# A gated mix of linear attention and an MLP: the denominators' sums by exchanges of partitions on VectorE

## The chip, the core and the metric

The kernel runs on one core of a Trainium2 chip. The metric is the device time of one launch in microseconds. Engines by the names of the profile: PE is TensorE's matrix products, PEld its weight loads, DVE is VectorE, ACT is ScalarE, POOL is GpSimd, SP is the queue that starts most of the DMAs.

## The reference

Everything is float32. With x of 2048 rows and 448 columns, 16 heads of 28 columns, and an MLP of 1792 hidden columns:

```
g = sigmoid((x * gate_w).sum(-1))
q, k, v = x @ wqkv                       per head, 28 columns each
phi(t) = where(t > 0, t + 1, exp(t)) + 1e-6
kv = phi(k)^T v ;  z = sum over rows of phi(k)
a = ((phi(q) kv) / (phi(q) . z + 1e-6)) @ wo
b = relu(x @ w1 + b1)^2 @ w2 + b2
out = g * a + (1 - g) * b
```

What matters here is the denominator `phi(q) . z + 1e-6`: for each row of x and each head, a sum over the head's 28 columns.

## The kernel before

**Precision.** Each operand of a product is kept as two rounded parts, a high one (name ending in h) and a low one (l), made by `split_hi` (L63, a copy that rounds, on ScalarE or VectorE) and `split_lo` (L71, value minus high part, on VectorE or GpSimd). A product of two split operands is three products on TensorE: h with h, h with l, l with h. All add up in one PSUM bank.

**Tiling.** The 2048 rows are four blocks of 512 (`TB`), b = 0 to 3. The hidden columns are 14 groups of 128, f = 0 to 13. `up` (L241) makes one group of a block: 11 products of 512 columns into `h_ps`, then `hidden` (L231) empties it: ScalarE's relu with bias (L233) and square (L234) make `hr`, VectorE's cast (L69) makes `hh` and its subtraction (L72) `hl`. `down` (L260) multiplies `hh`, `hl` with w2 and adds into four `o_ps` banks, 12 products of 448 columns; with `leave` the last few are owed and run behind the next `up`, so that TensorE has work while a split is under way. The first product of a group reads `hh`, the third `hl`.

**First half** (L538 to L681): groups 0 to 6 for the blocks in turn, with the keys, their sums, and the product of keys and x from which, between the halves, the values' part is made. During it the mask `hm` (L664, L665) is loaded and rounded: 128 by 128, a one where two partitions belong to one head.

**Second half** (L684 to L771): groups 7 to 13 for the blocks in the order 3, 0, 1, 2; these four rounds are called the first to fourth pass here. Beside a pass's groups run the queries of the next block and the attention of this block:

- `queries` (L449 on): phi(q) for 512 rows as four tiles `qe` of 128 partitions, each from 11 products (7 for the fourth) into a bank `q_ps`. ScalarE's exp (L286) and VectorE's `qr` (L287) both read the bank; L288 joins them. The fourth tile holds only half as many columns, in two copies, and goes through DMAs that swap halves (`qv`, `qr`, L472 to L479). Each tile is multiplied with z, one number to a partition, and added into `ds` (L466, L468).
- The columns of q are dealt so that a head's part of `ds` lies in eight partitions of the same 32: those that agree in all bits of the partition's number but the bits 1, 2 and 16. The denominator is the sum over these eight.
- `split_den` (L483) splits `ds` into `dh` (ScalarE) and `dl` (VectorE). `denominators` (L489) multiplies both with the mask on TensorE: two products of 512 columns into the bank `d_ps`, which put the sum over a head's eight partitions into each of the eight. ScalarE adds 1e-6 on its way out (L494), and VectorE takes four reciprocals of 128 columns each (L498), in the next round of `run_todo`.
- `scaled` (L501): each tile `qe` times the reciprocals (L506), then split into `qh` and `ql`; the last tile by `split_last` (L76), which is longer.
- `attention` (L513): 11 products with `m_s` into a bank `a_ps` for each 128 rows; emptied by ScalarE (`u`, L525) and added to the rest by VectorE (L526). The tiles of q are taken in their order, so the last tile's `qh` and `ql` are used by the tenth and eleventh product.
- `finish` (L275): VectorE's L278 makes 128 rows of `out`, and SP sends them.

`q_ps`, `d_ps` and `a_ps` share two PSUM banks that alternate (`bank`, L48): each new tile waits until the tile two before it has been read out.

**What sets the order.** The order on TensorE, ScalarE and VectorE is the program's (L170): each runs its instructions in the order of the text, and waits at the first whose data are not there. Steps put on the list `todo` run in the next `run_todo` (L530), ahead of the next group's `up`.

Of the kernel before, what the change touches and what calls it, by code (L numbers as in the profile page):

```python
# [7 lines left out]
F = mybir.dt.float32  # L8
R = mybir.dt.float32r
AF = mybir.ActivationFunctionType  # L10
# [5 lines left out]
P = 128  # L16
# [12 lines left out]

@with_exitstack  # L30
def gated_mix_kernel(ctx: ExitStack, tc: tile.TileContext, xw, xt, xn, wk, wq, wv, wo, w1a, w1b, w2, b1, b2, gw,
                     hmask, kvmask, halves, out):
    nc = tc.nc
    act, dve, pool, pe, sp = nc.scalar, nc.vector, nc.gpsimd, nc.tensor, nc.sync

# [18 lines left out]
    def slot(shape, dt, name):  # L54
        return work.tile(shape, dt, name=name, tag="s", bufs=NSLOT)
# [7 lines left out]
    def split_hi(eng, hi, src):  # L63
        if eng is act:
            act.activation(hi, src, AF.Copy)  # L65
        elif eng is pool:
            pool.tensor_scalar(hi, src, 1.0, 0.0, op0=ALU.mult, op1=ALU.add)
        else:
            eng.tensor_copy(hi, src)  # L69

    def split_lo(eng, lo, src, hi):  # L71
        eng.tensor_tensor(lo, src, f32(hi), op=ALU.subtract)  # L72
# [131 lines left out]

    b2_s = keep.tile([P, D], F, name="b2_s")
    gw_s = keep.tile([P, D], F, name="gw_s")
    hm = keep.tile([P, 8 + P], R, name="hm")[:, 8:]
    dve.memset(ones, 1.0)
    ksum = keep.tile([P, D], F, name="ksum")

# [269 lines left out]
            after()  # L480
        return [swap if c == 3 else after]

    def split_den(b):  # L483
        den[b, "h"], den[b, "l"] = slot([P, TB], R, f"dh{b}"), slot([P, TB], R, f"dl{b}")
        total = den.pop((b, "s"))
        split_hi(act, den[b, "h"], total)
        split_lo(dve, den[b, "l"], total, den[b, "h"])

    def denominators(b):  # L489
        ps = bank(f"d_ps{b}")  # L490
        products(ps, [(hm, den.pop((b, "h"))), (hm, den.pop((b, "l")))])
        den[b, "r"] = rec = slot([P, TB], F, f"rec{b}")

        act.activation(rec, ps, AF.Copy, bias=1e-6)  # L494

        def part_(i):
            for j in range(2 * i, 2 * i + 2):
                dve.reciprocal(rec[:, j * P:(j + 1) * P], rec[:, j * P:(j + 1) * P])  # L498
        return [lambda: part_(0), lambda: part_(1)]
# [119 lines left out]
    for b in range(1, NB):  # L619
        for f in range(NH):  # L620
            leave = leaves[b][f]
            run_todo()
            up(b, f)
            if f == 0:
                down(b - 1, NH - 1)
                half_done(b - 1)
                if b == 1:
                    for c in range(1, 4):
                        todo += gram(0, c)
                        run_todo()  # L630
            else:
                down(b, f - 1, leave=leave)
            if f == 1:
                todo += late_keys
                run_todo()
            if f == 0:
                load_xn(4 * b)
            if f < 4:
                if f < 3:
                    load_xn(4 * b + f + 1)  # L640
                if f == 0 and leave:
                    late_keys = keys(4 * b, leave)
                else:
                    late_keys = []
                    todo += keys(4 * b + f)
            elif f < 6:
                todo += gram(b, f - 4)
            else:
                todo += gram(b, 2)
                run_todo()  # L650
                todo += gram(b, 3)
            if b + 1 < NB:
                if 1 <= f < 5:
                    load_x(b + 1, f - 1)
                if 3 <= f:
                    split_x(b + 1, f - 3)
            if b == 2:
                if f < 4:
                    load_wq(f)
                if 1 <= f < 5:  # L660
                    split_wq(f - 1)
                if f == 5:
                    raw = slot([P, P], F, "hmr")
                    pool.dma_start(out=raw, in_=hmask)  # L664
                    split_hi(act, hm, raw)  # L665
                    load(half, halves)
            if b == 3:
                if f < 4:
                    load_w1(1, 0, f)
                if f == 4:  # L670
                    for c in range(4):
                        split_w1(1, 0, c)
                if f >= 2:
                    load_w2(NH + f - 2)
                if f >= 3:
                    split_w2(NH + f - 3)
                if f == 5:
                    key_sums()
                if f >= 5:
                    load_kv(2 * f - 10)  # L680
                    load_kv(2 * f - 9)  # L681
# [5 lines left out]
    for n, b in enumerate(order):  # L687
        then = order[n + 1] if n + 1 < NB else None
        for f in range(NF - NH, NF):
            fl = f - NH  # L690
            run_todo()
            if fl == (0 if n else 4) and n != 1:
                split_den(b)
            up(b, f)
            if then is not None and n and fl < 2:
                load_x(then, 2 * fl)
                load_x(then, 2 * fl + 1)
            if n == 0:
                if 1 <= fl < 3:
                    load_x(then, 2 * fl - 2)  # L700
                    load_x(then, 2 * fl - 1)
                if fl == 1:
                    for c in range(4):
                        split_w1(1, 1, c)
                    for j in range(2, 4):
                        load_wo(j)
                if 1 <= fl < 5:
                    split_wo(fl - 1)
                if fl < 2:
                    load_w2(NH + 5 + fl)  # L710
                if fl < 3:
                    split_w2(NH + 4 + fl)
                if 2 <= fl < 4:
                    split_x(then, 2 * fl - 4)
                    split_x(then, 2 * fl - 3)
            elif then is not None and 1 <= fl < 3:
                split_x(then, 2 * fl - 2)
                split_x(then, 2 * fl - 1)
            if fl:
                if n + 1 < NB or f + 2 < NF:  # L720
                    down(b, f - 1, leave=leaves[n][fl])
                elif f + 1 < NF:
                    down(b, f - 1, range(3))
                    down(b, f - 1, [3], leave=leaves[n][fl], end=NH - 3)
            elif n == 0:
                down(b, NH - 1)
                half_done(b)
            else:
                down(order[n - 1], NF - 1)
                for i in range(4):  # L730
                    if n == 1:
                        attention(order[0], i)
                        if i == 1:
                            split_den(b)
                    finish(order[n - 1], i)
            if n == 0:
                if fl in (2, 3):
                    m_product(fl - 2)
                if fl < 4:
                    todo += queries(b, (3, 0, 1, 2)[fl])  # L740
                if fl == 0:
                    for c in range(4):
                        load_w1(1, 1, c)
                    raw = kv_product()
                    phase1.close()
                    late = ctx.enter_context(tc.tile_pool(name="late", bufs=1, side="right", reuse_waits="tile"))
                    m_s = keep.tile([P, 7, D], R, name="m_s", tag="wkm", bufs=1)
                    split_kv(raw)
                    for j in range(2):
                        load_wo(j)  # L750
                if fl == 4:
                    m_product(2)
                if fl == 5:
                    m_product(3)
                for c in ((0,), (1, 2, 3))[fl - 5] if fl >= 5 else ():
                    scaled(b, c)
                if fl >= 4:
                    for c in ((3,), (0,), (1, 2))[fl - 4]:
                        todo += queries(then, c)
                if fl == 4:  # L760
                    todo += denominators(b)
            else:
                if fl == 0:
                    todo += denominators(b)
                if 2 <= fl < 4:
                    scaled(b, 2 * fl - 4)
                    scaled(b, 2 * fl - 3)
                for i in (((0,), (1,), (2, 3)) if then is not None else ((0, 1), (2,), (3,)))[fl - 4] if fl >= 4 else ():
                    attention(b, i)
                if then is not None and 3 <= fl:  # L770
                    todo += queries(then, (3, 0, 1, 2)[fl - 3])  # L771
# [70 lines left out]
```

## Time and profile before

| what | value |
|---|---|
| time, median of 3 runs | 434.96 us (434.93 to 435.02) |
| span of the profiled execution | 432.7 us |
| TensorE's products, busy | 428.9 us |
| VectorE, busy | 284.7 us, 464 instructions |
| ScalarE, busy | 174.8 us, 304 instructions |
| GpSimd, busy | 72.0 us |

The profile has one execution's span, from its first to its last instruction; a run's time is longer by what lies around it, 2.3 us with the median of the runs. A row of the timeline has the start in us from the span's begin, the length in us, the engine, the kernel's line, the operation, and what is written from what; "x4" is four in a row, and in brackets stands how long the engine sat idle before it and what it waited for. A line such as L72 is a helper's, so rows are told apart by the names of the tiles.

### The profile page before, as it was taken

Reading aid. Unit: us, or ns where it says so; the run is one execution under the profiler, and the core shown is the slowest. Engines: PE = TensorE matmul, PEld = TensorE weight load, DVE = VectorE, ACT = ScalarE, POOL = GpSimd, SP = SyncE. Lnnn points to the kernel's source line nnn. Section 1 sums busy time; section 2 is a strip of 40 time slices with the busy share of each in tenths; the row PEclk is TensorE's granted clock in tenths of the full one; section 3 lists DMA queues with packets and bytes.
Section 4 is the critical chain, followed back from the end, with each engine's and each line's share of the span. In section 5 each row is a group of like instructions: output and inputs, shape, how many; then the busy total and the mean of one; then the engine's idle time right before and its main releaser. Section 6 shows DMA issues by size and latency. Waiting matters only on the chain.

```text
span 432.7 us, 5576 instructions
## 1 busy us (share of the span) xinstructions
PE 428.9 (99%) x2058; PEld 380.6 (88%) x2058; DVE 284.7 (66%) x464; ACT 174.8 (40%) x304; POOL 72.0 (17%) x93
## 2 busy tenths in 40 slices
PE   9999999999999999999999999999999999999997
PEld 6889999898989899898898888988888888888986
DVE  5999518843499337884459777887653966457624
ACT  6855324521346133453145543444433534233421
POOL 0055006500065002540010441000100001000000
PEclk9999999999999999999999999999999999999999
DMA  8842302120232211223245321130101401002002
GB/s 284 240 134 63 96 0 71 24 68 5 65 89 63 68 45 48 66 59 110 65 117 144 72 63 38 63 120 0 26 0 46 139 0 27 0 0 86 0 2 85
DMA packets 18411, 29.11 MB, mean 67 GB/s; under 512 B 2896, under 2 KB 12736, under 8 KB 18384
## 3 DMA queue, kind: packets, MB, share of 16 engines
q1 hardware_dynamic: 16480, 26.46, 20.1%
q0 software_dynamic: 1760, 2.20, 2.3%
q8 instruction: 16, 0.26, 0.3%
q14 instruction: 11, 0.09, 0.1%
q10 hardware_dynamic: 144, 0.10, 0.1%
HBM read 22.43 MB, written 3.67 MB: 60 GB/s over the span
## 4 chain that ended last, share of the span: by engine, by line
PE 99%; DVE 0%; issue 0%
PE h_ps L229 32%; PE o_ps L254 31%; PE q_ps L84 8%; PE a_ps L84 8%; PE g_ps L84 8%; PE k_ps L254 8%; PE kv_ps L404 1%; PE warm_ps L177 1%; PE m_ps L84 1%; PE d_ps L84 0%; PE last L84 0%; PE h_ps L549 0%; PE z_ps L398 0%; DVE last L786 0%
## 5 line engine op out<-in xcount | busy, mean ns | idle before, releaser
L254 PE MATMUL o_ps<-w,hh 128*128 128x448 f32 x444 | 127.9, 362 | 0.0
L229 PE MATMUL h_ps<-xh,w 128*128 128x512 f32 x390 | 124.7, 390 | 0.0
L254 PEld LDWEIGHTS o_ps<-w,hh 128*128 128x128 f32 x444 | 83.2, 187 | 7.6
L229 PE MATMUL h_ps<-xl,w 128*128 128x512 f32 x224 | 86.7, 389 | 0.0
L229 PEld LDWEIGHTS h_ps<-xh,w 128*128 128x128 f32 x390 | 73.1, 188 | 14.7 <-DVE w L72 0.4
L254 PE MATMUL o_ps<-w,hl 128*128 128x448 f32 x222 | 80.4, 362 | 0.0
L233 ACT ACTIVATE hr<-h_ps,b_s 128x512 f32<-128x512 f32 x56 | 38.1, 680 | 85.8 <-PE h_ps L229 80.3
L69 DVE CAST hh<-hr 128x512 fp32r<-128x512 f32 x56 | 23.5, 420 | 61.3 <-ACT hr L234 61.1
L229 PEld LDWEIGHTS h_ps<-xl,w 128*128 128x128 f32 x224 | 42.0, 188 | 7.9
L254 PEld LDWEIGHTS o_ps<-w,hl 128*128 128x128 f32 x222 | 41.6, 188 | 3.7
L72 DVE TENSOR_TENSOR hl<-hr,hh 128x512 fp32r<-128x512 f32 x56 | 39.6, 707 | 3.4
L72 POOL TENSOR_TENSOR nl<-xnr,nh 128x384 fp32r<-128x384 f32 x16 | 17.2, 1075 | 119.0 <-ACT nh L65 118.9
L234 ACT ACTIVATE hr<-hr 128x512 f32<-128x512 f32 x56 | 35.4, 632 | 1.8
L84 PE MATMUL q_ps<-xh,wq_s 128*128 128x512 f32 x100 | 33.0, 389 | 0.0
L84 PE MATMUL a_ps<-m_s,qh 128*128 128x448 f32 x112 | 32.7, 362 | 0.0
L254 PE MATMUL k_ps<-wk_s,xh 128*128 128x448 f32 x112 | 32.7, 361 | 0.0
L475 POOL DMA_DIRECT2D qr<-qv x16 | 7.9, 503 | 124.3 <-ACT qv L472 94.5
L72 DVE TENSOR_TENSOR pl<-r,ph 128x448 fp32r<-128x448 f32 x16 | 23.7, 1479 | 0.0
L326 POOL TENSOR_TENSOR ksum<-ksum,r 128x448 f32<-128x448 f32 x15 | 23.3, 1554 | 1.1 <-DVE r L288 1.1
L84 PE MATMUL q_ps<-xl,wq_s 128*128 128x512 f32 x60 | 23.3, 389 | 0.0
L254 PE MATMUL k_ps<-wk_s,xl 128*128 128x448 f32 x64 | 23.2, 363 | 0.0
L84 PE MATMUL a_ps<-m_s,ql 128*128 128x448 f32 x64 | 23.2, 362 | 0.0
(118 smaller groups left out, 571.0 us busy)
## 6 DMA issues: line engine op xcount, KB each, us to landing
xr<-in_xt SPq DMA_DIRECT2D x27, 256.0 KB, 2.7
xnr<-in_xn SPq DMA_DIRECT2D x16, 224.0 KB, 2.6
out<-out SPq DMA_DIRECT2D x15, 224.0 KB, 2.0
w2r<-in_w SPq DMA_DIRECT2D x14, 224.0 KB, 2.7
w1r<-in_w1a SPq DMA_DIRECT2D x7, 256.0 KB, 2.8
w1r<-in_w1b SPq DMA_DIRECT2D x8, 192.0 KB, 3.3
m_s<-m POOLq DMA_DIRECT2D x12, 112.0 KB, 2.5
wqr<-in_wq SPq DMA_DIRECT2D x4, 256.0 KB, 2.7
```

The lines of the kernel that those rows point to most:

```text
L69: eng.tensor_copy(hi, src)
L72: eng.tensor_tensor(lo, src, f32(hi), op=ALU.subtract)
L84: pe.matmul(out_ps, a, b, start=(i == 0), stop=(i == n - 1))
L177: pe.matmul(warm_ps[:, :256], warm[:, :P], warm, start=True, stop=True)
L229: pe.matmul(ps, a, m, start=(c == 0 and n == 0), stop=(c == 3 and n == 1))
L233: act.activation(r, ps, AF.Relu, bias=b1_s[:, f:f + 1])
L234: act.activation(r, r, AF.Square)
L254: pe.matmul(ps, a, m, start=start, stop=stop)
L326: pool.tensor_tensor(ksum, ksum, p, op=ALU.add)
L404: pe.matmul(kv_ps[:JE, js], wv_s[c][:, js], gsum[c][:, js], start=(c == 0), stop=(c == 3))
L475: pool.dma_start(out=r[p + 16:p + 32], in_=v[p:p + 16])
```

## The change

The eight rows' sum is made on VectorE. For each of the steps 16, 1 and 2, an exchange writes into a new tile `dt` the rows of `ds` with the partition numbers p and p xor step swapped, inside each 32 partitions, and an addition puts the two together. The last addition is one instruction with the 1e-6 and writes `rec`; the four reciprocals follow as before.

`split_den` with `dh` and `dl`, both products with the mask, the bank `d_ps`, ScalarE's copy out of it, and the mask's load and rounding are gone. A tile of the same size as `hm` keeps its place in memory.

The place changes too. `denominators` now issues its six VectorE instructions at once where it is called; before, it issued the products there. In the first, third and fourth pass it is called where it was. In the second pass it is called one group later, and all four `scaled` of that pass come at the fourth group (fl = 3), where two were at the third and two at the fourth.

```diff
-    def split_den(b):
-        den[b, "h"], den[b, "l"] = slot([P, TB], R, f"dh{b}"), slot([P, TB], R, f"dl{b}")
-        total = den.pop((b, "s"))
-        split_hi(act, den[b, "h"], total)
-        split_lo(dve, den[b, "l"], total, den[b, "h"])
-
     def denominators(b):
-        ps = bank(f"d_ps{b}")
-        products(ps, [(hm, den.pop((b, "h"))), (hm, den.pop((b, "l")))])
-        den[b, "r"] = rec = slot([P, TB], F, f"rec{b}")
-
-        act.activation(rec, ps, AF.Copy, bias=1e-6)
+
+        total, other, rec = den.pop((b, "s")), slot([P, TB], F, f"dt{b}"), slot([P, TB], F, f"rec{b}")
+        for step in (16, 1, 2):
+            dve.stream_shuffle(other, total, [p ^ step for p in range(32)])
+            if step != 2:
+                dve.tensor_tensor(total, total, other, op=ALU.add)
+        dve.scalar_tensor_tensor(rec, total, 1e-6, other, op0=ALU.add, op1=ALU.add)
+        den[b, "r"] = rec
...
-                    raw = slot([P, P], F, "hmr")
-                    pool.dma_start(out=raw, in_=hmask)
-                    split_hi(act, hm, raw)
...
-            if fl == (0 if n else 4) and n != 1:
-                split_den(b)
...
-                        if i == 1:
-                            split_den(b)
...
-                if fl == 0:
+                if fl == (n == 1):
                     todo += denominators(b)
-                if 2 <= fl < 4:
-                    scaled(b, 2 * fl - 4)
-                    scaled(b, 2 * fl - 3)
+                for c in range(4) if n == 1 and fl == 3 else range(2 * fl - 4, 2 * fl - 2) if n > 1 and 2 <= fl < 4 else ():
+                    scaled(b, c)
```

More of the change, by code (lines that the diff above doesn't have):

```diff
@@ L31, in gated_mix_kernel @@
 def gated_mix_kernel(ctx: ExitStack, tc: tile.TileContext, xw, xt, xn, wk, wq, wv, wo, w1a, w1b, w2, b1, b2, gw,
-                     hmask, kvmask, halves, out):
+                     kvmask, halves, out):
     nc = tc.nc
@@ L206, in gated_mix_kernel @@
     gw_s = keep.tile([P, D], F, name="gw_s")
-    hm = keep.tile([P, 8 + P], R, name="hm")[:, 8:]
+    keep.tile([P, 8 + P], R, name="off")
     dve.memset(ones, 1.0)
@@ L806 @@
                            for j in range(NJ)])
-    hmask = (head[:, None] == head[None, :]).astype(np.float32)
     kvmask = (np.arange(JE)[:, None] // DH == k_of[None, :] // DH % 4).astype(np.float32)
@@ L828 @@
         "gw": inputs["gate_w"],
-        "hmask": hmask,
         "kvmask": kvmask,
```

## The prediction

> **What bounds the kernel now.** I read the page first: span, engines, chain of what ended last, then who made TensorE wait.
>
> ```profile
> span 432.7 us, 5576 instructions
> PE 428.9 (99%) x2058; PEld 380.6 (88%) x2058; DVE 284.7 (66%) x464; ACT 174.8 (40%) x304; POOL 72.0 (17%) x93
> PE 99%; DVE 0%; issue 0%
> PE warm_ps L177 <- PEq L834: 0.8, 1, 0.8
> ```
>
> TensorE is the chain: 99% of the span, and the list of waits holds a single one for it, 0.8 us at the very start. So a product taken away is time gained, and any wait put in front of a product is time lost in full, since nothing on TensorE can swallow it. VectorE is busy 66% of the span, but its share says nothing of when it is late; that must come from the timeline where its results are due.
>
> The groups (line, engine, operation | busy us, mean ns | idle before) give what the change touches:
>
> ```profile
> L84 PE MATMUL d_ps<-dl,hm 128*128 128x512 f32 x4 | 1.6, 389 | 0.0
> L72 DVE TENSOR_TENSOR dl<-ds,dh 128x512 fp32r<-128x512 f32 x4 | 2.8, 691 | 2.1 <-ACT dh L65 2.1
> L65 ACT ACTIVATE dh<-ds 128x512 fp32r<-128x512 f32 x4 | 2.5, 630 | 6.9 <-DVE ds L468 6.9
> L494 ACT ACTIVATE rec<-d_ps 128x512 f32<-128x512 f32 x4 | 2.4, 597 | 3.5 <-PE d_ps L84 3.5
> L72 DVE TENSOR_TENSOR hl<-hr,hh 128x512 fp32r<-128x512 f32 x56 | 39.6, 707 | 3.4
> ```
>
> **Gain.** Eight products go, two in each of four passes. A product lasts 389 ns but they overlap; what counts is the step from start to start:
>
> ```profile
> 250.83 0.39 PE L84 MATMUL d_ps<-dh,hm 128*128 128x512 f32 x1
> 251.29 0.39 PE L229 MATMUL h_ps<-xh,w 128*128 128x512 f32 x1
> ```
>
> Two products take 251.29 - 250.83 = 0.46 us, so TensorE gains about 0.45 us in each pass, 1.8 us in all. ScalarE loses dh and rec (0.63 and 0.60 us a pass); it is 40% busy, so that counts only where VectorE waits behind it, below. The load of the mask and its split lie in the first half beside TensorE's unbroken work: 0.
>
> **Price of the chain.** In each pass VectorE loses dl (0.69) and gets three exchanges, two additions and one addition with the constant, each waiting for the one before. An addition of this size takes 0.69 (row dl). From one dependent instruction to the next there is a step of 0.73:
>
> ```profile
> 331.94 0.69 DVE L288 SCALAR_TENSOR_TENSOR qe<-qe,qr 128x512 f32<-128x512 f32 x1
> 332.67 0.75 DVE L468 SCALAR_TENSOR_TENSOR ds<-qe,zc,ds 128x512 f32<-128x512 f32 x1
> ```
>
> The trace has no exchange of partitions. The bound below is the cast of the same size in the next view (row 335.36, 0.43); the bound above, the 0.75 of the ds row plus 0.25 for an unseen setting-up instruction, an estimate, 1.0 together. I take 0.69, the plain one-column-a-step pass of rows hl and dl, so the chain is L = 6 x 0.73 = 4.4 us; by the ends, 3.6 to 5.3.
>
> The Trainium skill ("VectorE: DVE Perf Modes", section on the perf-mode tier table) gives a shuffle only the 1x mode and about 2400 ns at 2048 columns, beside 2293 for an fp32 tensor_tensor. By that page the exchange would be some 0.1 us dearer than an addition (an estimate: 0.80), L 4.7 and the result 1.3 us later than mine; no run here shows it yet.
>
> **Third and fourth pass (blocks 1 and 2).** VectorE's order becomes: hh, hl of group 7; four out; chain; four reciprocals; hh, hl of group 8. The second product group of TensorE that follows needs this hh and hl.
>
> ```profile
> 332.88 0.37 PE L254 MATMUL o_ps<-w,hh 128*128 128x448 f32 x1
> 333.99 0.67 ACT L233 ACTIVATE hr<-h_ps,b_s 128x512 f32<-128x512 f32 x1
> 335.36 0.43 DVE L69 CAST hh<-hr 128x512 fp32r<-128x512 f32 x1 [0.55 <-ACT hr L234]
> 336.43 2.46 DVE L278 SCALAR_TENSOR_TENSOR out<-o_ps,gate,part 128x448 f32<-128x448 f32 x4
> 338.63 0.57 PE L254 MATMUL o_ps<-w,hh 128*128 128x448 f32 x2
> 338.83 0.69 ACT L233 ACTIVATE hr<-h_ps,b_s 128x512 f32<-128x512 f32 x1 [1.89 <-PE h_ps L229]
> 338.80 3.38 DVE L498 RECIPROCAL rec<-rec 128x128 f32<-128x128 f32 x4
> 342.09 0.36 DVE L69 CAST hh<-hr 128x512 fp32r<-128x512 f32 x1
> 342.49 0.69 DVE L72 TENSOR_TENSOR hl<-hr,hh 128x512 fp32r<-128x512 f32 x1
> 343.94 0.36 PE L254 MATMUL o_ps<-w,hl 128*128 128x448 f32 x1
> ```
>
> 1. Without dh, hr of group 7 starts 0.2 after o_ps (as 338.83 after 338.63): 333.08 instead of 333.99, 0.9 earlier. hh follows 1.37 later (333.99 to 335.36), hl 0.46 after it, and 0.61 after hl the four out begin, at 335.5. They take 2.37 (336.43 to 338.80) and end at 337.9: 0.9 won.
> 2. Chain to 342.3; reciprocals 3.29 (338.80 to 342.09) to 345.6; hh 0.40 (342.09 to 342.49); hl from 346.0 to 346.7, where it ended at 343.18.
> 3. TensorE uses hl at 343.94, now 0.45 earlier: 343.49. From the end of hl to the product I allow 0.25 (a weight load of 0.19 and a signal), so the product starts at 346.9. **Stall 3.4 us**, L - 1.0.
>
> Behind this hl nothing is late beyond TensorE's own delay: VectorE then waited for ScalarE, and that idle time takes up the rest. Net of the 0.45: +3.0 in the third pass. The fourth has the same order around the chain: +3.0.
>
> **First pass (block 3).** The chain stands in front of work with more room; the wait comes 25 us later.
>
> ```profile
> 249.44 0.55 ACT L65 ACTIVATE m<-m_ps 128x448 fp32r<-128x448 f32 x1
> 250.60 0.62 DVE L72 TENSOR_TENSOR m<-m_ps,m 128x448 fp32r<-128x448 f32 x1
> 252.12 3.39 DVE L498 RECIPROCAL rec<-rec 128x128 f32<-128x128 f32 x4 [0.90 <-ACT rec L494]
> 257.94 0.62 DVE L72 TENSOR_TENSOR m<-m_ps,m 128x448 fp32r<-128x448 f32 x1 [1.35 <-ACT m L65]
> 258.48 0.68 DVE L506 TENSOR_TENSOR qe<-rec,qe 128x512 f32<-128x512 f32 x1
> 261.57 0.37 PE L254 MATMUL o_ps<-w,hh 128*128 128x448 f32 x1
> 273.22 0.68 DVE L287 TENSOR_SCALAR qr<-q_ps 128x512 f32<-128x512 f32 x1
> 274.27 0.56 PE L84 MATMUL a_ps<-m_s,qh 128*128 128x448 f32 x2
> ```
>
> Without dl, m can follow its ScalarE half at 250.02; 0.54 later the chain starts, at 250.56, ends at 254.9, the reciprocals at 258.2. Then hh 0.46, hl 0.61, m 0.54 (257.94 to 258.48): qe starts at 259.86, 1.38 late. From there to qr VectorE waits only inside its own chains, so the 1.38 stays. qr (of the next block's second query tile) empties the PSUM bank that a_ps takes: two banks alternate, and d_ps was one step of both. qr ends at 275.28, a_ps can start at 275.53, TensorE would be there at 273.82: **stall 1.7**, L - 2.7. Net +1.25. The hidden products in between have room: hh and hl of group 12 are done by about 259.3 and due in the o_ps group that starts at 261.57 - 0.45.
>
> **Second pass (block 0).** Here the chain is moved behind hh, hl of group 8 and two xl, and all four scalings behind group 10.
>
> ```profile
> 286.21 0.69 ACT L233 ACTIVATE hr<-h_ps,b_s 128x512 f32<-128x512 f32 x1 [1.82 <-PE h_ps L229]
> 289.69 1.28 DVE L72 TENSOR_TENSOR xl<-xr,xh 128x512 fp32r<-128x512 f32 x2
> 296.22 0.36 PE L254 MATMUL o_ps<-w,hl 128*128 128x448 f32 x1
> 295.36 0.68 DVE L506 TENSOR_TENSOR qe<-rec,qe 128x512 f32<-128x512 f32 x1
> 297.35 0.68 DVE L506 TENSOR_TENSOR qe<-rec,qe 128x512 f32<-128x512 f32 x1
> 303.11 0.68 DVE L506 TENSOR_TENSOR qe<-rec,qe 128x512 f32<-128x512 f32 x1
> 305.37 0.69 DVE L72 TENSOR_TENSOR ql<-qe,qh 128x512 fp32r<-128x512 f32 x1
> 306.71 0.36 PE L84 MATMUL a_ps<-m_s,ql 128*128 128x448 f32 x1
> ```
>
> hr of group 8 starts at 286.21 - 0.45 = 285.76, hh 1.37 later, hl 0.46 after it, and 0.61 for it and for each of the two xl: the chain goes from 289.4 to 293.8, the reciprocals to 297.1, hh and hl of group 9 to 298.2. The product on that hl was at 296.22 and would be at 295.77; it can start at 298.45: **stall 2.7**, L - 1.7. After hl come three x instructions (2.0 together) and hh, hl of group 10 (1.07), so scaling begins at 301.2. A tile's scaling takes 297.35 - 295.36 = 1.99, the last one 2.95 (303.11 to 306.06, the end of ql); 3 x 1.99 + 2.95 = 8.9, so the last ql ends at 310.1. Its product at 306.71 would be at 306.71 - 0.45 + 2.7 = 308.96 and can start at 310.35: **a second stall of 1.4**, whatever L, because in the kernel before two of the four tiles were scaled ahead of group 10's hh. Net -0.45 + 2.7 + 1.4 = +3.65.
>
> **Sum.** 1.25 + 3.65 + 3.0 + 3.0 = +10.9 us, as a formula about 4L - 6.7. The span goes from 432.7 to 443.6. Around the span lie 434.96 - 432.7 = 2.3 us; I leave them: **445.9 us**, +2.5%.
>
> **Rivals.**
> - *VectorE's idle third hides the chain*, and the products' 1.8 us are the whole effect: 433.2, faster. For it: 66% busy, and each pass does carry idle time after the chain (1.35 us ahead of m). Against: the third and fourth pass stand still from L = 1.0 on, and the three additions alone make 2.2; with free exchanges the formula, without the first pass's stall, still gives +2.5. It turns at an L of about 1.4. Chance 0.03; another 0.02 for landing within 0.2%.
> - *TensorE comes back from a stall at half rate.* The start of the trace shows one:
>
> ```profile
> 0.78 3.14 PE L177 MATMUL warm_ps<-const-bfloat16-1.0 128*128 128x256 bf16 x14 [0.78 <-PEq L834]
> ```
>
>   14 products of 256 columns in 3.14 us are 0.224 each, as long as the 0.23 of 512 columns later. Four microseconds of that cost 2 us; after the two 3.4 us stalls, +4: 449.9. For it the stalls' length, against it that only a start from rest shows it. The Trainium skill ("TensorE: Matmul & The Clock Gate", Part 1) lets the clock fall after one idle window of about 3.4 us that runs freely; by that a gap of 3.4 us would seldom hold a whole one. Chance 0.12.
> - *Only the late hidden products wait*, and the two stalls ahead of attention (1.7 and 1.4) are taken up by idle time that I have not seen: 442.8. Against: both are sums over an in-order engine. Chance 0.08.
>
> **How the numbers follow.** Forecast 0.75. L from 3.6 to 5.3 gives +7.7 to +14.5: 442.7 to 449.5. With the third rival at one end and part of the half rate at the other, 442.5 to 451. A measurement here can tell about 0.2%: faster 0.03, same 0.02, slower 0.95.
>
> **What would show it.** d_ps gone and 2050 products in the page; exchanges in the groups near 0.7 us; TensorE with about 13 us of waits on hl or hh (L72, L69) in the second, third and fourth pass, on q_ps's qr in the first, and one on ql in the second; product steps unchanged after stalls. I am wrong if TensorE's waits stay under 2 us, if an exchange costs far from 0.7, or if the waits lie elsewhere.

## The result, and the profile after

The changed kernel takes 450.11 us (median of six runs, 447.22 to 451.48), the kernel before on the same chip 435.08 (434.93 to 435.4, six runs): a ratio of 1.0337 with the 95% interval [1.0312, 1.0361]. It is slower by 15.0 us where 11 were forecast. The time is inside the range, 4.2 us above the forecast, and within 0.2 us of what the second rival gave.

The page of the changed kernel, the lines that answer to those shown of before, and at the end of the fence its list of waits of TensorE:

```profile
span 449.3 us, 5572 instructions
PE 436.1 (97%) x2050; PEld 385.2 (86%) x2050; DVE 298.9 (67%) x496; ACT 170.9 (38%) x295; POOL 71.8 (16%) x92
PEclk9999999999999999999999999989999699997999
PE 85%; DVE 11%; ACT 2%; issue 1%; DVEq 0%; ACTq 0%
PE o_ps L254 <- DVE hh L69: 8.0, 3, 2.9
PE a_ps L84 <- DVE qr L287: 1.4, 1, 1.4
PE warm_ps L177 <- PEq L821: 0.8, 1, 0.8
```

Two things stand in it. VectorE, which had 0% of the chain that ended last, has 11% now, and TensorE waits for it in four places, 9.4 us in all. That is the forecast's mechanism. But TensorE is also busy for 436.1 us with 2050 products, 7.2 us more than before with 2058. The row PEclk says why: its digits 8, 6 and 7 are slices in which the granted clock was below full. So there are two losses: time in which TensorE stands, and time in which it runs at half rate.

The exchange itself, in the instructions of the tile `dt` (count, then shortest, median and longest duration in ns), and the ends of the first pass's chain on VectorE's timeline:

```profile
L487 DVE STREAM_SHUFFLE dt<-ds x12: 725/730/748, 250.9 to 404.5; 128x512 f32<-128x512 f32 x12
```

```profile
250.86 0.72 DVE L487 STREAM_SHUFFLE dt<-ds 128x512 f32<-128x512 f32 x1
...
255.34 0.95 DVE L495 RECIPROCAL rec<-rec 128x128 f32<-128x128 f32 x1
```

An exchange takes 0.73 us where I took 0.69, and the chain from its first exchange to the first reciprocal takes 255.34 - 250.86 = 4.48 us where I took L = 4.4.

The third pass, on the timeline of the changed kernel:

```profile
340.95 2.46 DVE L278 SCALAR_TENSOR_TENSOR out<-o_ps,gate,part 128x448 f32<-128x448 f32 x4
...
343.33 0.73 DVE L487 STREAM_SHUFFLE dt<-ds 128x512 f32<-128x512 f32 x1
...
347.83 3.39 DVE L495 RECIPROCAL rec<-rec 128x128 f32<-128x128 f32 x4
...
348.30 0.37 PE L254 MATMUL o_ps<-w,hl 128*128 128x448 f32 x1
...
351.13 0.36 DVE L69 CAST hh<-hr 128x512 fp32r<-128x512 f32 x1
351.53 0.69 DVE L72 TENSOR_TENSOR hl<-hr,hh 128x512 fp32r<-128x512 f32 x1
...
351.55 1.12 PE L254 MATMUL o_ps<-w,hh 128*128 128x448 f32 x2 [2.89 <-DVE hh L69]
...
355.45 0.63 PE L229 MATMUL h_ps<-xh,w 128*128 128x512 f32 x1
...
355.88 0.63 PE L229 MATMUL h_ps<-xl,w 128*128 128x512 f32 x1
```

The order is the one worked out: four out, chain, four reciprocals, then hh and hl of group 8, and TensorE waits for them. The next product starts 351.55 - 348.30 = 3.25 us after the last one instead of a step of 0.20, a stall of 3.05. Behind it the products are not what they were: from one of 512 columns to the next are 355.88 - 355.45 = 0.43 us, nearly twice the 0.23 of before.

To see how long that lasts, here are windows of 3.41 us around the gaps of the changed kernel. (A row has the window, its length, the busy time of TensorE's products, weight loads, VectorE, ScalarE and GpSimd with their counts, then the granted clock, DMA share and GB/s. The edges are laid on the instant at which the clock changes, which a row of finer windows gave.)

```profile
272.41:275.82 3.41, 1.99 (x11) 1.53 (x10) 2.47 (x5) 2.90 (x5) 0.00 (x0) 1.00 0.20 26
275.82:279.23 3.41, 3.41 (x18) 3.13 (x19) 3.31 (x5) 0.64 (x1) 0.00 (x0) 1.00 0.33 128
296.31:299.72 3.41, 1.20 (x6) 0.67 (x4) 3.38 (x6) 1.32 (x2) 0.00 (x0) 1.00 0.00 0
299.72:303.13 3.41, 3.41 (x10) 2.81 (x9) 3.34 (x7) 0.00 (x0) 0.00 (x0) 0.50 0.00 0
303.13:306.54 3.41, 3.41 (x16) 2.85 (x16) 2.01 (x4) 1.27 (x2) 0.00 (x0) 1.00 0.00 0
347.51:350.92 3.41, 1.16 (x6) 0.64 (x4) 3.38 (x5) 3.38 (x7) 0.00 (x0) 1.00 0.34 110
350.92:354.33 3.41, 2.78 (x8) 2.36 (x8) 3.27 (x7) 0.13 (x1) 0.00 (x0) 0.50 0.00 0
354.33:357.74 3.41, 3.41 (x10) 2.83 (x9) 2.79 (x5) 0.55 (x1) 0.00 (x0) 0.50 0.01 2
357.74:361.15 3.41, 3.41 (x18) 3.02 (x17) 2.05 (x4) 1.93 (x4) 0.00 (x0) 1.00 0.00 0
```

The granted clock is 0.50 for exactly one such window after the second pass's gap and for exactly two after the third's; the fourth pass is as the third. The starts lie at 299.72, 350.92 and 408.95: 51.20 and 58.03 us apart, 15 and 17 times 3.413. After the first pass's gap of 1.4 us the clock stays at 1.00. Five half-rate windows cost 5 x 3.41 / 2 = 8.5 us of product time, less 0.7 for the 1.4 us in which TensorE stood in them anyway: 7.8.

The sum: products gone, -1.8; stalls of 1.6, 2.4, 3.05 and 3.05 (each from product to product, less one step; the second is the step from 296.75 to 299.33), +10.1; half rate, +7.8. That is 16.1 of the 16.6 us between the two spans.

The spread of the runs is this too. The three runs at 450.7 to 451.5 us have a mean granted clock of 0.981, the two at 449.0 and 449.5 have 0.989, the one at 447.2 has 0.995: five, three and about one such window.

### The profile page after: what moved, and what is told of

It reads as the page before. It is cut to its first block, busy times and chain, and to the rows that moved or that the text cites. A ratio compares the mean times of both kernels' runs of the same rounds, so it can differ in the third digit from the quotient of the medians.

```text
span 449.3 us, 5572 instructions
## 1 busy us (share of the span) xinstructions
PE 436.1 (97%) x2050; PEld 385.2 (86%) x2050; DVE 298.9 (67%) x496; ACT 170.9 (38%) x295; POOL 71.8 (16%) x92
## 4 chain that ended last, share of the span: by engine, by line
PE 85%; DVE 11%; ACT 2%; issue 1%; DVEq 0%; ACTq 0%
PE h_ps L229 27%; PE o_ps L254 26%; PE a_ps L84 8%; PE k_ps L254 8%; PE g_ps L84 8%; PE q_ps L84 6%; DVE rec L495 3%; DVE dt L487 2%; DVE ds L489 1%; DVE out L278 1%; PE kv_ps L404 1%; PE warm_ps L177 1%; DVE rec L490 1%; DVE ql L72 1%; DVE qe L503 1%
## 5 line engine op out<-in xcount | busy, mean ns | idle before, releaser
L254 PE MATMUL o_ps<-w,hh 128*128 128x448 f32 x444 | 132.1, 373 | 8.0 <-DVE hh L69 8.0
L229 PE MATMUL h_ps<-xh,w 128*128 128x512 f32 x390 | 126.3, 395 | 0.0
L254 PEld LDWEIGHTS o_ps<-w,hh 128*128 128x128 f32 x444 | 85.8, 194 | 16.9 <-DVE hh L69 9.2
L229 PE MATMUL h_ps<-xl,w 128*128 128x512 f32 x224 | 87.8, 394 | 0.0
L229 PEld LDWEIGHTS h_ps<-xh,w 128*128 128x128 f32 x390 | 74.6, 192 | 14.6
L254 PE MATMUL o_ps<-w,hl 128*128 128x448 f32 x222 | 82.6, 372 | 0.0
L229 PEld LDWEIGHTS h_ps<-xl,w 128*128 128x128 f32 x224 | 42.9, 191 | 8.1
L254 PEld LDWEIGHTS o_ps<-w,hl 128*128 128x128 f32 x222 | 42.8, 193 | 4.7 <-DVE hl L72 0.9
L523 DVE SCALAR_TENSOR_TENSOR part<-part,gate,u 128x448 f32<-128x448 f32 x16 | 10.9, 683 | 20.2 <-ACT u L522 20.2
L84 PEld LDWEIGHTS a_ps<-m_s,qh 128*128 128x128 f32 x112 | 20.9, 187 | 3.4 <-DVE qr L287 1.8
```

Of the source, the lines that this page charges most:

```text
L84: pe.matmul(out_ps, a, b, start=(i == 0), stop=(i == n - 1))
L229: pe.matmul(ps, a, m, start=(c == 0 and n == 0), stop=(c == 3 and n == 1))
L254: pe.matmul(ps, a, m, start=start, stop=stop)
L523: dve.scalar_tensor_tensor(part[t], part[t], gate[:, 1, t:t + 1], u, op0=ALU.mult, op1=ALU.add)
```

## The experiments

**Theory A**: the chain of additions and exchanges stands on VectorE ahead of work that TensorE soon needs, TensorE stands still where forecast, and the gaps of some 2 us and more bring the half rate behind them. Against it stand B (the half rate comes from something else than the gap, or the extra 4 us from something else than the half rate), C (the exchange is what costs, the rest of the change being free), D (idle time takes up the first pass's lateness) and, later, E and F (VectorE's amount of work is the bound, or only the reciprocals' place is).

### Filling the gaps

The changed kernel with unread products put into the gaps, so that TensorE is late but not idle:

```diff
+            if fl == 3 and n == 1 or fl == 2 and n > 1:
+                ps = bank(f"fill{b}")
+                for _ in range(20 if n == 1 else 26):
+                    pe.matmul(ps[:, :256], warm[:, :P], warm, start=True, stop=True)
```

> The changed kernel with products that nothing reads put where TensorE stands still (20 of 256 columns in the second pass, 26 each in the third and fourth), so that it is late but not idle. Theory A (the waits behind the chain on VectorE, and half rate after each long idle gap): the waits stay, the half rate goes; 1.6 + 2.7 + 1.4 + 3.5 + 3.5 - 1.8 = 10.9 us over the kernel before, 446.0 us (445.2 to 446.8), mean clock 1.000, runs within 0.5 us of each other. Rival B (the half rate comes from something else than the idle gap, such as the exchanges): 449 to 451 us as now, clock about 0.98 to 0.99.

Measured: 445.95 us (445.63 to 446.43, four runs), ratio to before 1.0254 [1.0239, 1.027]. With 72 products more the kernel is some 4 us faster (its ratio to before is 1.0254, the changed kernel's 1.0337). From its windows, one where the changed kernel ran at half rate, and from its timeline the second pass's attention:

```profile
350.00:354.00 4.00, 3.95 (x25) 3.10 (x23) 3.86 (x8) 1.08 (x2) 0.00 (x0) 1.00 0.00 0
```

```profile
310.41 0.37 PE L84 MATMUL a_ps<-m_s,ql 128*128 128x448 f32 x1
311.35 0.48 PE L84 MATMUL a_ps<-m_s,qh 128*128 128x448 f32 x1 [0.57 <-DVE qh L78]
312.08 0.47 PE L84 MATMUL a_ps<-m_s,ql 128*128 128x448 f32 x1 [0.25 <-DVE ql L72]
```

The clock stays at 1.00 there (the mean over the whole run is 0.999 to 1.000 in all four), and the time is the forecast's 445.9. So the forecast's sum is what this order of work costs at full rate, and the rest was the half rate. The second pass's second stall, on the last qh and ql, is here: two products that should be 0.20 behind the one before are 0.94 and 0.73 behind it, 1.3 us lost, 1.4 forecast. In the changed kernel no wait on ql is listed: the half rate ahead of it made TensorE late enough.

These rows also show how to read a list of waits: it counts from the end of a product that lasts 0.36 us while the next could start after 0.20, so each wait costs some 0.2 us more than its listed time, and a delay below that is not listed at all.

### The additions without the exchanges

Each addition adds the tile to itself, so the sum over a head's rows is left out:

```diff
...
-            dve.stream_shuffle(other, total, [p ^ step for p in range(32)])
             if step != 2:
-                dve.tensor_tensor(total, total, other, op=ALU.add)
-        dve.scalar_tensor_tensor(rec, total, 1e-6, other, op0=ALU.add, op1=ALU.add)
+                dve.tensor_tensor(total, total, total, op=ALU.add)
+        dve.scalar_tensor_tensor(rec, total, 1e-6, total, op0=ALU.add, op1=ALU.add)
```

> The changed kernel without its twelve exchanges: each addition adds the tile to itself, so the sums over a head's rows are left out. The chain is 2.2 us. Theory A: waits of 0 in the first pass, 0.5 + 1.4 in the second, 1.2 and 1.2 in the third and fourth, no gap long enough for half rate: 435.1 + 4.3 - 1.8 = 437.6 us (437.0 to 438.4), clock 1.000. Rival C (the exchanges themselves carry the loss, the additions being hidden): 433.3 us.

Measured: 437.19 us (437.01 to 437.33), ratio 1.0052 [1.0037, 1.0067], clock 1.000, with listed waits of 1.1 us on hh (two of 0.5) and 0.9 on qh and ql, each some 0.2 dearer than listed, and delays on hl behind them. Against the 434.83 us of before, measured beside it, this is +2.4, where the prediction had +2.5 for free exchanges. C falls: with half the chain gone the kernel is still slower, since the three additions alone are more than the order has room for.

### The change in the first pass alone, and in the third and fourth alone

The kernel before, with the new sum for some blocks only (`EX = [3]` for the first pass, `EX = [1, 2]` for the third and fourth; `exchanged` is the changed kernel's `denominators`):

```diff
     def denominators(b):
+        if b in EX:
+            return exchanged(b)
...
-            if fl == (0 if n else 4) and n != 1:
+            if fl == (0 if n else 4) and n != 1 and b not in EX:
                 split_den(b)
```

> The kernel before, with the exchanges in the first pass alone (block 3). Theory A: two products gone (-0.45) and one wait of 1.6 us ahead of attention, 25 us behind the chain: 436.2 us (435.9 to 436.5), clock 1.000, since this gap is short. Rival D (idle time of VectorE takes up a chain that stands so far ahead): 434.65 us.

Measured: 436.46 us (436.26 to 436.57, five runs), ratio 1.0036 [1.0022, 1.005], clock 0.999, and one new wait of TensorE, 1.4 us of a_ps on qr. It is the stall that the prediction followed through 25 us of VectorE's chain; D falls. In the timeline the step is 1.77 us, a stall of 1.6. Less the 0.45 us of two products that makes 1.1 (the prediction has 1.25), while the time is 1.6 longer; the rest isn't followed here, but the profiled run has a wait of 0.8 us far from the change, in the first half, that the profile of before doesn't have (h_ps on ScalarE's w).

> The kernel before, with the exchanges in the third and fourth pass alone. Theory A: in each -0.45 + 3.5 = +3.05 from the wait on hl, and up to 2 us of half rate behind it: 441.2 us with no spell of half rate, 443 with one, 445.3 with two; the clock tells which (about 0.987 with two). Rival B (half rate from the exchanges, whatever TensorE does) gives the same two spells here, so this run only sizes them; a time under 440 would say that the forecast's waits are too large.

Measured: 443.27 us (442.55 to 444.08, four runs), ratio 1.0192 [1.0177, 1.0208]. Both gaps of the profiled run, 442.55 us long, are of the same length, 2.89 and 2.87 us, and only one is followed by half rate. Its windows, cut as above:

```profile
341.97:345.38 3.41, 1.66 (x8) 1.06 (x6) 3.34 (x6) 1.89 (x4) 0.00 (x0) 1.00 0.46 153
345.38:348.79 3.41, 2.22 (x10) 1.75 (x11) 3.31 (x6) 0.56 (x1) 0.00 (x0) 1.00 0.00 0
400.00:403.41 3.41, 1.20 (x5) 0.79 (x6) 3.27 (x7) 0.46 (x1) 0.00 (x0) 1.00 0.00 0
403.41:406.82 3.41, 3.41 (x10) 2.96 (x9) 2.44 (x4) 0.87 (x2) 0.00 (x0) 0.50 0.00 0
```

The first gap is cut by an edge into 1.75 and 1.19 us of standing, the second lies with 2.21 us in one window, and the next window is at half rate. Without its 1.7 us this run is 442.55 - 1.7 - 434.83 = 6.0 us above before, the forecast's 3.0 for each pass.

### The gap without the change

The kernel before, with nothing of the change, and six unread additions on VectorE ahead of the reciprocals in the third and fourth pass:

```diff
                 if fl == 0:
                     todo += denominators(b)
+                    if n > 1:
+                        idle = slot([P, D], F, f"idle{b}")
+                        for _ in range(6):
+                            dve.tensor_tensor(idle, b2_s, b2_s, op=ALU.add)
```

> The kernel before, products with the mask and all, with six additions that nothing reads (448 columns, 0.54 us a step, 3.3 us together) on VectorE ahead of the reciprocals of the third and fourth pass: a wait of TensorE without any exchange. Theory A: 0.5 of slack, so hl is 2.8 late in each and TensorE idle for 2.2: 435.0 + 5.6 = 440.6 us with the clock at 1.000, and up to 2 us more for each spell of half rate, which then comes from the gap alone; runs differ by such steps. Rival B (only exchanges bring half rate): 440.6 us in every run, clock 1.000.

Measured: 443.1 us (442.9 to 444.7, four runs), ratio 1.0196 [1.018, 1.0212], mean clock 0.996 in three runs and 0.992 in one. B falls: there is no exchange in this kernel, and the half rate is there. Its windows in the third and the fourth pass, two gaps of 2.63 us:

```profile
341.74:345.15 3.41, 2.34 (x11) 1.63 (x9) 3.34 (x6) 1.20 (x2) 0.00 (x0) 1.00 0.55 156
345.15:348.56 3.41, 1.79 (x8) 1.35 (x9) 3.38 (x7) 1.25 (x3) 0.00 (x0) 1.00 0.00 0
348.57:351.98 3.41, 3.41 (x10) 2.80 (x9) 3.27 (x7) 0.00 (x0) 0.00 (x0) 0.50 0.00 0
...
399.77:403.18 3.41, 1.78 (x8) 1.14 (x7) 3.38 (x6) 1.32 (x2) 0.00 (x0) 1.00 0.01 3
403.18:406.59 3.41, 2.36 (x10) 1.89 (x11) 3.27 (x6) 0.03 (x1) 0.00 (x0) 1.00 0.00 0
```

The same gap, once cut into 1.07 and 1.62 us of standing and followed by half rate, once into 1.63 and 1.05 and not. In the first the longer part lies behind the edge, at the start of its window, in the second ahead of it, at the end.

### Gaps of other lengths

The same edit with 4, 5 and 9 additions, to see what length the half rate needs.

> The kernel before with 4 unread additions of 128x448 (0.62 us each) on VectorE ahead of the first two reciprocals of the third and of the fourth pass, where the run before had 6 and an idle gap of 2.63 us in each pass. Nothing is left out. The gaps should be 2.63 - 2 x 0.62 = 1.4 us, and without half rate behind them the time 1.25 us a pass less than the 441.2 us that 6 additions give without a spell (443.0 less the one spell of 1.8 that its profile shows): 438.7. Theory W (half rate follows only where a gap holds a whole sampling window that runs freely and is longer than 1.4 and shorter than 2.6 us): 438.7, clock 1.000 in all runs. Theory Y (each gap of a microsecond or more has about the same chance of half rate, whatever its length): about half the gaps followed by it, 438.7 to 442.3, clock below 1.000 in most runs.

Measured: 439.2 us (438.61 to 439.41), ratio 1.009 [1.0075, 1.0105]; the longest wait is 1.3 us, and the mean clock is 1.000, 1.000, 1.000 and 0.999. No gap was followed by half rate: Y misses.

> The same with 5 unread additions: gaps of 2.63 - 0.62 = 2.0 us, 440.0 us without half rate. Theory W: between none and a few of the gaps followed by half rate, fewer than with 6 additions: 440.0 to 441.0. Theory Y: as many as with 6 additions, about half: 440.0 to 443.6, median near 441.8.

Measured: 443.08 us (441.7 to 443.62), ratio 1.0177 [1.0157, 1.0196]; gaps of 1.98 us, mean clock 0.992 in three runs and 0.995 in one. Here both theories miss: with two of them in most runs, half rate came more often than behind the longer gaps of 2.63 us. The profiled run shows both gaps:

```profile
343.50:346.91 3.41, 1.43 (x8) 0.89 (x6) 3.38 (x6) 2.43 (x4) 0.00 (x0) 1.00 0.36 123
346.91:350.32 3.41, 3.41 (x10) 2.70 (x9) 3.31 (x7) 0.02 (x1) 0.00 (x0) 0.50 0.00 0
...
401.55:404.96 3.41, 1.67 (x7) 1.25 (x8) 3.34 (x7) 0.84 (x2) 0.00 (x0) 1.00 0.00 0
404.96:408.37 3.41, 3.41 (x10) 2.79 (x9) 2.02 (x4) 1.26 (x2) 0.00 (x0) 0.50 0.00 0
```

> The same with 9 unread additions: gaps of 2.63 + 3 x 0.62 = 4.5 us, 441.2 + 3.7 = 444.9 us without half rate. Theory W: a gap of 4.5 us holds a whole window nearly always if the window is about 2 us: both gaps followed by half rate in nearly every run, 444.9 + 2 x 2 = about 449 us, with little spread, clock near 0.99 in all runs. Theory Y: about half the gaps, 445 to 449 with steps of 2 us between the runs, median near 447.

Measured: 449.52 us (448.75 to 449.79), ratio 1.0323 [1.0306, 1.0341], mean clock 0.985 to 0.988; gaps of 4.6 us, both followed by half rate, as W has it.

What goes with the half rate is not the gap's length but, outside a narrow range, how much of it falls into one window of a grid of 3.413 us. In the profiled runs, the end of a run left out, every window at full rate in which TensorE stood for 1.98 us or more was followed by half rate (ten, three of them in the run with interleaved scalings below), and none with 1.42 or less was. Between them lie four windows, near half of 3.41: those with 1.62 and 1.74 were followed by half rate, those with 1.63 and 1.75 were not, so there the amount alone doesn't decide. In the two that were followed, TensorE stands at the start of the window, in the other two at its end. If the clock changes 0.1 us or more behind the window on which that is decided, all four would lie on the right side of one limit; no run tests this. W named a sampling window, but took it to be shorter, and to need to be idle as a whole; both were wrong.

### Other orders on VectorE

The scalings of the changed kernel interleaved, so that the last ql is earlier (`scaled` takes several tiles; all are multiplied by the reciprocals first, then all are split):

```diff
+        for c in cs:
+            p = ps[c]
...
             dve.tensor_tensor(p, den[b, "r"], p, op=ALU.mult)
...
+        for c in cs:
+            h, lo = qs[c]
...
+            split_lo(dve, lo, ps[c], h)
```

> The changed kernel with the scalings of a pass interleaved: the multiplications of the tiles that belong to one step first, then their splits, so that VectorE doesn't stand waiting for ScalarE inside each tile. Theory A: the wait ahead of attention in the first pass goes (1.6 us; about 2 us of VectorE's waiting is saved there) and with it the second wait of the second pass (1.4, which shows only when no half rate hides it); the waits on hh and hl stay with their half rate: 447.0 us (444.5 to 449). Rival E (what counts is only how much work VectorE has, not where it stands still): no change, 450.

Measured: 448.58 us (444.44 to 449.16, four runs), ratio 1.0282 [1.0241, 1.0324]. The interval overlaps that of the changed kernel, since the number of half-rate windows in a run covers what the edit is worth: the run at 444.44 has a clock of 0.996, the others 0.981 to 0.985. Runs with the same clock can be compared: at 0.981 it takes 449.1 and 449.2, the changed kernel 450.7 to 451.5. Its list of waits has the three on hh, 8.0 us as in the changed kernel, and none of a_ps on qr any more. So the first pass's stall is gone with the amount of VectorE's work unchanged, which speaks against E.

The reciprocals of the changed kernel behind hh and hl of the next group:

```diff
+            held = [step for step in todo if step.__name__ == "<lambda>"]
+            todo[:] = [step for step in todo if step.__name__ != "<lambda>"]
...
+            for step in held:
+                step()
```

> The changed kernel with the four reciprocals behind hh and hl of the next group instead of ahead of them. Theory A: the waits on hh and hl shrink to 0.3 us, but the scalings come 3.3 us later for it, so that most of the loss comes back ahead of attention: first pass 1.6, second about 4, third and fourth about 2.3 each in several small waits; 435.0 - 1.8 + 10.2 = 443.4 us (441 to 446). Rival F (the order of reciprocals and hl is all that was wrong): 434.9 to 435.5 us, the first pass's wait alone being left.

Measured: 444.75 us (443.07 to 446.3, four runs), ratio 1.0225. F falls: the long wait on hh is gone but for 0.6 us, and eight others take its place, the first three of these lines on attention:

```profile
PE a_ps L84 <- DVE qh L78: 2.1, 2, 1.7
PE a_ps L84 <- DVE qr L287: 1.3, 1, 1.3
...
PE a_ps L84 <- DVE ql L72: 0.8, 3, 0.3
PE o_ps L254 <- DVE hh L69: 0.6, 1, 0.6
```

None is longer than 1.7 us, and the clock of the profiled run, 443.57 us long, is 1.000. Two of the four runs, with 445.9 and 446.3 us, have a clock of 0.992, so half rate is there too; what stood long enough in them isn't shown, as they have no profile.

Last, VectorE's work put where it has room. The first exchange with its addition goes ahead of hh of group 7 (in the second pass between two out), the rest of the chain where `denominators` stood, the reciprocals of the second to fourth pass behind hh and hl of group 8, and the scalings in interleaved pairs at the third and fourth group, as before the change:

```diff
+            held = [step for step in todo if n and step.__name__ == "<lambda>"]
+            todo[:] = [step for step in todo if step not in held]
...
+            if n > 1 and fl == 0:
+                exchange(b, 16)
...
+            for step in held:
+                step()
...
-                if fl == (n == 1):
-                    todo += denominators(b)
+                if fl == 0:
+                    todo += denominators(b, 1, 2)
+                if 2 <= fl < 4:
+                    scaled(b, 2 * fl - 4, 2 * fl - 3)
```

> The changed kernel with VectorE's order spread out by the slack of the timeline: in the second to fourth pass one exchange and addition of the chain ahead of the out (third and fourth: ahead of hh of group 7), the rest behind them, the reciprocals behind hh and hl of group 8, the second pass's scalings back at the third and fourth group, and scalings interleaved everywhere. Theory A: VectorE has room for all of it, no wait longer than 0.3 us is left on TensorE, and the eight products are the whole effect: 433.3 us (433.0 to 434.2), clock 1.000, faster than the kernel before. Rival E (VectorE has no room for 4.5 us more in these stretches whatever the order): 436 us or more.

Measured: 433.75 us (433.13 to 434.66, nine runs) beside 434.88 (434.54 to 435.21) of before, ratio 0.9976 [0.9967, 0.9986]: faster than both kernels. Its page and its list of waits:

```profile
span 432.1 us, 5577 instructions
PE 428.1 (99%) x2050; PEld 378.9 (88%) x2050; DVE 298.1 (69%) x496; ACT 170.3 (39%) x295; POOL 71.5 (17%) x92
PEclk9999999999999999999999999999999999999999
```

```profile
PE warm_ps L177 <- PEq L840: 0.8, 1, 0.8
```

VectorE does the same 298 us of work as in the changed kernel, in the same 496 instructions, and no wait of a product on it is listed. So E falls too: what cost 15 us was not the amount of the work but its place. Its timelines of VectorE and of TensorE in the third pass:

```profile
339.87 0.69 DVE L495 SCALAR_TENSOR_TENSOR rec<-ds,dt 128x512 f32<-128x512 f32 x1
341.90 0.43 DVE L69 CAST hh<-hr 128x512 fp32r<-128x512 f32 x1 [1.35 <-ACT hr L234]
```

```profile
342.08 0.37 PE L254 MATMUL o_ps<-w,hl 128*128 128x448 f32 x1
342.38 0.67 PE L254 MATMUL o_ps<-w,hh 128*128 128x448 f32 x2
343.11 0.47 PE L254 MATMUL o_ps<-w,hl 128*128 128x448 f32 x1
343.42 0.57 PE L254 MATMUL o_ps<-w,hh 128*128 128x448 f32 x2
```

The chain ends 1.35 us before hh of group 8 can be made. Of the 1.8 us that eight products are worth, 1.1 is seen in the time, and 0.6 between the spans of the two profiles, 432.7 and 432.1. What is missing there is lost in delays too short for the list of waits. The last four rows have steps of 0.30, 0.73 for two and 0.31 instead of 0.20, 0.40 and 0.20, so 0.54 us lost, and the products on the next group's hl and hh, from 347.52 on, lose 0.6 more in the same way.

## Why the prediction was right, and where it was short

- **TensorE is the chain, so products are worth their step, and every wait is lost in full.** Right. At 1.8 us, the gain is hidden in the changed kernel and shows, for the larger part, only where all waits are gone.
- **L = 4.4.** Measured 4.48. The exchange is 0.73 us, near the value chosen, not near the upper end. The Trainium skill ("VectorE: DVE Perf Modes", the perf-mode tier table) has a shuffle a little dearer than an fp32 addition; the trace agrees in the sign, 0.73 against 0.69, with less than the 0.80 that I worked out from its figures. I had added the Trainium skill's whole difference at 2048 columns to an addition of 512 columns; an estimate by its ratio, 2400 to 2293, is 0.72, near the 0.73 of the trace. The setting-up instruction, for which the upper bound allowed 0.25, is there (LOAD_MASK_SELECT) and takes 0.014.
- **First pass, stall 1.7 on qr.** Measured 1.6, and 1.6 in the timeline of the kernel with the change there alone. Tracing one delay through an engine that works in order gave the right place 25 us on.
- **Second pass, 2.7 and then 1.4.** The first was 2.4, and the list names hh rather than hl, because hh itself was late; the product follows 0.06 us behind hh's end (298.91 + 0.36 to 299.33), where 0.25 was allowed behind hl's. The second shows only where the half rate is taken away, with 1.3.
- **Third and fourth pass, 3.4 each.** Measured 3.05 each until the product on hh, which also waits; I had counted to the one on hl. In the kernel with the change in these passes alone, where the third pass ran at full rate, hl brings 0.4 more, 3.5 together.
- **"Product steps unchanged after stalls."** This is the step that failed. Steps were nearly twice as long for 3.41 us after one stall and for 6.83 us after each of two others, +7.8 us. The forecast itself, 445.9, has nothing for this; the measured time is inside the range because part of the half rate was put into its upper end, 451. The range from L alone ended at 449.5.
- **The second rival, chance 0.12.** It had the mechanism and was set aside for two reasons that don't hold. One was that only a start from rest shows a half rate: a trace without gaps can't show what follows a gap. The other was that a gap of 3.4 us would seldom hold a whole window. A gap of 2 us suffices. The rival's price, +4 for two stalls, was also too low: by the steps that are longer than before, the half rate cost 1.9, 3.0 and 2.9 us behind three stalls. That its 449.9 lies so close to the 450.1 comes partly from errors that cancel: the stalls on hh and hl, whose last part passes under the half rate, and the second stall of the second pass, which is gone.
- **VectorE's idle third hides the chain.** Refuted for this order. With VectorE's work spread it is nearly true: the idle third was there, but elsewhere.
- **Only the late hidden products wait.** Refuted: the wait on qr is there, and that on ql with the gaps filled.

What stays open: where between 1.42 and 1.98 us of standing the limit lies, and what decides at 1.62 to 1.75. And a window at half rate was followed by another when TensorE stood in it for only 0.63 us, and never when it didn't stand; where the edge lies in such a window was not tried.

## What to carry to other kernels

When work goes from a full engine to a half idle one, ask where in the order it stands, not how much it is: list what waits behind it there and when that is due. The same instructions cost 15 us in one place and gained 1 in another. And behind a stall of TensorE of about 2 us or more, allow for 1.7 to 3.4 us lost at half rate, which may come or not; if the time of a kernel jumps in such steps from run to run, look at the granted clock first.

## What the runs showed of the hardware

- The granted clock changes on a grid of 3.413 us that runs through the whole execution: starts of half rate in one trace lie 15 and 17 grid steps apart, and spells last 3.41 or 6.83 us. The Trainium skill ("TensorE: Matmul & The Clock Gate", Part 1) gives a free-running window of that length, and the traces agree. Its rule that the rate falls after at least one idle window does not agree: about half a window of standing is enough, 1.98 us or more in all ten cases seen and 1.62 to 1.75 in two of four.
- Whether a gap of 2 to 3 us is followed by half rate goes with where the grid cuts it: gaps of about 2.9 and of 2.63 us went both ways in a single trace. The grid lies otherwise in each run: counted from the span's start, the half rate begins at 299.72 us in one profile and at 348.57 in another, 14.3 grid steps apart.
- Unread products in the gaps kept the clock at 1.00 in the window shown, and the mean clock of the runs at 0.999 to 1.000; they were worth some 4 us.
